# Batch 0's rows and spectra with the 32 slots innermost, batch 1's first stage moved behind the last stage of batch 0's transform, idle products on TensorE up to layer 1, and the last pieces of w2 decoded later

## The chip, the cores and the metric

The kernel runs on one core of one Trainium2 chip. The metric is the time of one execution on the device in microseconds (us); lower is better. Three runs of the kernel before took 1601.73, 1601.77 and 1603.76 us, so the median is 1601.77 us. The execution that the profiler recorded took 1600.86 us by the same clock.

The engines are called PE (TensorE, matrix products; its weight loads are PEld), DVE (VectorE), ACT (ScalarE), POOL (GpSimd) and SP (SyncE, which issues nearly all transfers). PSUM is the memory that PE writes and that ACT and DVE read; SBUF is the memory that all engines work from. A "unit-stride" walk reads neighbouring elements of a partition one after the other; a "strided" one jumps.

## The reference

Eight sequences of 3136 tokens with 256 features go through two parts, all in float32:

```
X  = rfft(x, axis=1)
Yr = Xr @ w_r - Xi @ w_i + b_r
Yi = Xr @ w_i + Xi @ w_r + b_i
Y  = soft_threshold(Yr, 0.01) + 1j * soft_threshold(Yi, 0.01)
y  = irfft(Y, n=3136)
u  = y + (y.T @ U @ V).T        # U: 3136 x 32, V: 32 x 3136
out = u + relu(u @ w_ch1) @ w_ch2   # 256 -> 1024 -> 256
```

U, V, w_ch1 and w_ch2 arrive as 64-bit floats and the kernel turns their words into float32 itself ("decoding").

## The kernel before, in words

**The stages.** The transform of 3136 = 49 x 64 points is done as small matrix products. For each batch, stage A is a product over 49 rows, stage B a product with twiddles (25 row pairs, called slots, which are handled two at a time), then the mix (the 256 x 256 products with w_r and w_i, bias and threshold), then C (the inverse of B) and D (the inverse of A, together with the product with U). The product with V and two layers follow: layer 1 (l1_chunks, seven products by a scheme that saves one of eight) and layer 2 (l2_chunks). Layer 1 and 2 run in 49 windows of 512 tokens, six per batch and one for what is left. While the windows of batch b run, the stages of batch b+1 are put between them. Most float32 products are done as three products of a high and a low part.

**Batch 0 is special.** It has no windows of an earlier batch to run beside. a_first (line 689) loads the rows of batch 0 in six pieces and does 16 products of 512 columns, each of which leaves 32 slots x 16 features in one PSUM bank. DVE turns each bank in blocks of 32 x 32 (STREAM_TRANSPOSE) into t0t (line 665), which is kept in SBUF. In t0t the feature index is innermost: one slot's 128 features are neighbours, so b_early and b_mm (lines 832, 843) load a slot as PE weights at unit stride, and the transposes write at a stride of 128 elements. C (c_unit, line 1002) writes its spectra back to t0t, features innermost, by a copy on ACT (line 1012). z_turn (line 1100) then turns t0t in 16 transposes of 512 elements into zz; it reads and writes at strides of 128 or 64 elements. D of batch 0 (d_unit, line 1122) loads 64 neighbouring features of zz as weights, 256 products, each in two passes on PE. Its 12 units (6 groups of rows times 2 halves of the features) write two PSUM banks each; ACT copies them to xq, DVE adds up the U part in pa.

**What is shared.** The tiles t0t and w1t (weights of layer 1) share one region of SBUF (tag "w1"), x3w, zz0 and w2t (weights of layer 2) another ("w2"). So w1t can be written only when z_turn has read t0t, and w2t only when D has read zz0.

**Other work at the start.** decode (line 1230) turns one piece of 512 words in about a dozen instructions on ACT, DVE and, for w2, POOL. decoding (line 1480) goes through V, U, the four pieces of w1, combine (line 1442, which makes the seven weight tiles of w1t) and the four pieces of w2; steps(n) takes n of its steps. make_ud (line 1375) makes the product of U with the inverse table: 128 small products and, on ACT, 24 small copies to du, which D reads. Stage A of batch 1 (a_mm, line 724; eight units in two halves of four) loads xt, does four tiled products per unit and writes the result to DRAM (gd), from where stage B of batch 1 loads it. a_half has its two halves recorded at 95 and 133 on the scale of line 1537.

**What sets the order.** Nothing runs in the order in which it is written. Each instruction is recorded with a cost (cost, line 195), dependencies and a place; order and forward (lines 263, 391) simulate the five engines, take at each moment the ready instruction with the earliest due time, and trace (line 529) emits each engine's queue in that order. Where forward expects a gap on PE ahead of the first product into a PSUM tile, it fills it with products of the identity with itself (line 540) into that tile; these are called idle products here, and they are planned only in the first 200 us. Line 545 makes each POOL tensor operation wait for the DVE operation on SBUF before it in the plan, since the two share ports.

**From D to layer 1.** p_spread and p_unit (lines 1190, 1198) reduce pa, turn it on PE and split it into pt. u_prep (line 1603) of window 0 then multiplies pt with V (psv), adds this to xq, forms differences in tt, and splits them into high parts on ACT (oah, obh, och, odh) and low parts on POOL (oal, obl, ocl, odl). Layer 1 starts on these.

Of the kernel before, what the change touches and what calls it, by code (L numbers as in the profile page):

```python
# [27 lines left out]
NI = 32  # L28
# [13 lines left out]
STEPS_W = 8  # L42
# [119 lines left out]
class _Op:  # L162
    __slots__ = "n eng name args kw out cost lag move port mode group lead fill start preds succs unit at".split()


class _Program:


    def __init__(self):
        self.ops = []  # L170
        self.group = None

# [22 lines left out]
    def cost(self, op, out, ins):  # L195
# [22 lines left out]
        elif op.eng == "act":  # L218
            op.cost = 0.062 + 0.000844 * n + (0.036 if sb else 0) + (0.098 if "bias" in op.kw else 0)
            op.lag = 0.2  # L220
# [42 lines left out]
    def order(self):  # L263
# [66 lines left out]
        for k, u in enumerate(units):  # L330
            u[0].fill = fill.get(k, 0)
            for op in u:
                op.start = starts[k] + op.at
# [57 lines left out]
    def forward(self, units, size, tags, gap, late):  # L391
# [52 lines left out]
        self.idle = []  # L444
        starts, fill = [0.0] * len(units), {}
        while done < len(units):
# [42 lines left out]
            if e == "pe":  # L489
# [4 lines left out]
                gap_, each = t - max(free[e], b.granted) - 0.2, 0.222  # L494
                if done_pe == 0:
# [3 lines left out]
                fill[k] = max(0, int(gap_ / each)) if b.first[0] is u and t < FILL else 0  # L499
# [29 lines left out]
    def trace(self, engines, junk, tc):  # L529
# [4 lines left out]
        for op in sorted(self.ops, key=lambda o: (o.start, o.n)):  # L534
            if op.fill:
                o = op.out.buf.get()
# [14 lines left out]
def fft_mix_moe_kernel(  # L551
# [28 lines left out]
    def psm(shape, name):  # L580

        turn_m[0] += 1
        k = turn_m[0] % 3
        return (ps_m if k < 2 else ps_o).tile(shape, F32, tag=("psm0", "psm1", "pso0")[k], name=name)

    def banks(turn, name):

        pools = ((ps_f, "psf"),) * 2
        if turn % 4 == 1:
            pools = (ps_m, "psm0"), (ps_m, "psm1")  # L590
        elif turn % 4 == 3:
            pools = (ps_o, "pso0"), (ps_o, "pso1")
# [65 lines left out]
    w1t = const.tile([128, 7, 2, 512], F32R, name="w1t", tag="w1")  # L658
# [6 lines left out]
    t0t = const.tile([128, 57 * 128], F32, name="t0t", tag="w1")  # L665
    t0 = [t0t[:, 3200 * h : 3200 * h + 4096].rearrange("p (k d) -> p k d", k=32) for h in range(2)]
# [22 lines left out]
    def a_first():  # L689
# [10 lines left out]
        for k, xt in enumerate(parts):  # L700
            ps = ps_f.tile([128, 512], F32, tag="psf", name=f"psa_0_{k}").rearrange("p (i d) -> p i d", i=NI)
            pe.matmul(ps, lhsT=fa0, rhs=xt, start=True, stop=True)
# [4 lines left out]
            dve.transpose(out=t0[h][:, :, d : d + 16].rearrange("p k d -> p d k"), in_=ps.rearrange("p i d -> p d i"))  # L707
# [16 lines left out]
    def a_mm(b, c, loads=()):  # L724
# [33 lines left out]
    def a_spread(b, lo, hi, behind=12):  # L758
        us = []
        for half in range(2):  # L760
# [31 lines left out]
    def load_fb(b, q):  # L792
# [5 lines left out]
        else:  # L798
            fbt = mp.tile([128, 2, 128], F32, tag="oc" + "hl"[q % 2], name=f"fb_{b}_{q}")
# [202 lines left out]
    def c_unit(b, q):  # L1002
# [97 lines left out]
    def z_turn(h, m):  # L1100
        if m == 0 and h == 0:
            t = const.tile([128, NI, 128], F32, name="zz0", tag="w2")
            zz.extend([t[:, :, 0:64], t[:, :, 64:128]])
        elif m == 0:
            zz.append(const.tile([128, NI, 64], F32, name="zz2", tag="wm"))
        elif m == 4 and h == 1:
            zz.append(qp.tile([128, NI, 64], F32, tag="xq", name="zz3", bufs=3))
# [14 lines left out]
    def d_unit(b, t, du, loads=(), hs=(0, 1)):  # L1122
# [75 lines left out]
    def p_unit(b):  # L1198
# [8 lines left out]
        pt = qp.tile([128, D], F32R, tag="pt", name=f"pt_{b}")  # L1207
# [22 lines left out]
    def decode(name, hi=None, lo=None, full=None):  # L1230
# [6 lines left out]
        q, lf, p2 = [  # L1237
            mp.tile([128, 512], U32, tag="sv", name="d%s_%s%d%d" % (tag, *name), bufs=4)[:pp, :n]
            for tag in "mlp"
        ]  # L1240
# [94 lines left out]
    def setup_w(wrs=wrs, wis=wis, wt=wt):  # L1335

        dve.scalar_tensor_tensor(
            out=wt, in0=wrs, scalar=-1.0, in1=wis, op0=ALU.mult, op1=ALU.subtract
        )
# [35 lines left out]
    def make_ud(t):  # L1375
        n0, n = UNITS_D[t]
        ps = psm([128, 512], f"psu_{t}")
        parts = [(64 * j + 32 * r, K1 * j + 25 * r, 25 - r) for j in range(2) for r in range(2)]
        for k in range(n):
            for p, c, m in parts:  # L1380
                pe.matmul(
# [7 lines left out]
                )  # L1389
        for p, _, m in parts:  # L1390
# [138 lines left out]
    for half in range(2):  # L1529
        loads = []  # L1530

        def load(c, half=half, loads=loads):
            loads += a_load(1, 4 * half + c)

        for c in range(4):
            on((92, 129)[half] + c / 10, load, c)
        on((95, 133)[half], lambda half=half, loads=loads: a_half(1, half, loads + [s_state["c"]]))
    on(99.5, wait_2)
    for n in range(16):
        on(100.5 + 2 * n, steps, 1)  # L1540

    def turn():
        steps(100)
# [59 lines left out]
    def u_prep(w):  # L1603
# [4 lines left out]
        lo_eng = pool  # L1608
# [4 lines left out]
        def pair(tag, src, n=2):  # L1613
# [3 lines left out]
                else mp.tile([128, HT], F32R, tag=f"oc{k}", name=f"{tag}{k}_{w}")  # L1617
# [27 lines left out]
        def s1():  # L1645
            sub(dve, tv[:, 0], b_[0][1], b_[0][0])
            sub(dve, tv[:, 1], b_[1][1], tv[:, 0])
            hl["a"] = pair("oa", tv)

        def s2():  # L1650
            hl["b"] = pair("ob", x[:, :, 0:8])
# [188 lines left out]
    for st in u0:  # L1840
        st()
    setup_w()
# [164 lines left out]
```

## Time and profile before

| | |
|---|---|
| median of three runs | 1601.77 us |
| the profiled execution, its time | 1600.86 us |
| its span, from the first to the last instruction | 1599.0 us |
| PE busy | 1573.2 us, 98% |
| DVE busy | 1278.7 us, 80% |
| ACT busy | 942.1 us, 59% |
| POOL busy | 441.2 us, 28% |
| share of PE in the chain that ended last | 87% |

The busy time of PE contains the idle products, so a busy PE is not always one at work. A row of the table by stretches gives the stretch, its length, busy time and number of instructions of each engine, the granted clock of TensorE as a share of 2.4 GHz (0.5 is 1.2 GHz), and what the transfer engines did. A float32 product that is not split runs as two passes, and each pass is one instruction in the trace.

### The profile page before, as it was taken

Reading aid. Unit: us, or ns where it says so; the run is one execution under the profiler, and the core shown is the slowest. Engines: PE = TensorE matmul, PEld = TensorE weight load, DVE = VectorE, ACT = ScalarE, POOL = GpSimd, SP = SyncE. Lnnn points to the kernel's source line nnn. Section 1 sums busy time; section 2 is a strip of 40 time slices with the busy share of each in tenths; the row PEclk is TensorE's granted clock in tenths of the full one; section 3 lists DMA queues with packets and bytes.
Section 4 is the critical chain, followed back from the end, with each engine's and each line's share of the span. In section 5 each row is a group of like instructions: output and inputs, shape, how many; then the busy total and the mean of one; then the engine's idle time right before and its main releaser. Section 6 shows DMA issues by size and latency. Waiting matters only on the chain.

```text
span 1599.0 us, 37615 instructions
## 1 busy us (share of the span) xinstructions
PE 1573.2 (98%) x14586; PEld 1415.6 (89%) x14586; DVE 1278.7 (80%) x2486; ACT 942.1 (59%) x1998; POOL 441.2 (28%) x417
## 2 busy tenths in 40 slices
PE   8989999999999999999999999999999999999998
PEld 6957899899889889899888988999978999999997
DVE  7878898679977788678986889768986789866775
ACT  3856666566655666556655666556665566554553
POOL 1305343133312333223331333223321233312221
PEclk9979999999999999999999999999999999999999
DMA  9655254617674454715574365523656134520332
GB/s 227 199 146 152 72 180 133 153 55 180 172 194 116 126 149 113 176 30 143 155 206 125 98 178 146 131 81 96 163 152 193 29 95 120 125 67 14 82 61 39
DMA packets 220501, 202.73 MB, mean 127 GB/s; under 512 B 127590, under 2 KB 192408, under 8 KB 220244
## 3 DMA queue, kind: packets, MB, share of 16 engines
q1 hardware_dynamic: 217686, 199.47, 46.6%
q8 instruction: 115, 1.88, 0.5%
q10 hardware_dynamic: 2638, 0.86, 0.3%
q14 instruction: 62, 0.51, 0.1%
HBM read 123.69 MB, written 78.60 MB: 127 GB/s over the span
## 4 chain that ended last, share of the span: by engine, by line
PE 87%; DVE 7%; issue 2%; ACT 1%; DMA 1%; POOL 0%; SPq 0%; DVEq 0%; ACTq 0%; POOLq 0%
PE pso L542 30%; PE psy L542 18%; PE psx L542 8%; PE psq L542 6%; PE psb L542 5%; PE psd L542 5%; PE psa L542 4%; PE psz L542 4%; PE psc L542 3%; PE pst L542 3%; DVE ys L542 1%; PE psv L542 1%; DVE zz L542 1%; DVE tb L542 1%; DVE rl L542 1%
## 5 line engine op out<-in xcount | busy, mean ns | idle before, releaser
L542 PE MATMUL pso<-rh,w2t 128*128 128x512 f32 x1568 | 405.4, 381 | 0.0
L542 PEld LDWEIGHTS pso<-rh,w2t 128*128 128x128 f32 x1568 | 274.4, 190 | 26.5
L542 PE MATMUL pso<-rl,w2t 128*128 128x512 f32 x784 | 233.3, 379 | 0.0
L542 POOL TENSOR_TENSOR yl<-ys,yh 128x512 fp32r<-128x512 f32 (+1 forms) x94 | 121.4, 1292 | 223.8 <-ACT yh L542 88.1
L542 ACT ACTIVATE rh<-s 128x512 fp32r<-128x512 f32 x196 | 122.3, 629 | 78.7 <-DVE s L542 74.5
L542 PEld LDWEIGHTS pso<-rl,w2t 128*128 128x128 f32 x784 | 148.2, 189 | 21.0
L542 DVE SCALAR_TENSOR_TENSOR rl<-s,rh 128x512 fp32r<-128x512 f32 x196 | 149.7, 767 | 18.4 <-ACT rh L542 16.2
L542 DVE SCALAR_TENSOR_TENSOR ys<-tb,rl 64x256 f32<-64x256 f32 x350 | 151.9, 434 | 14.7 <-ACT rl L542 9.4
L542 POOL TENSOR_TENSOR tl<-ts,th 128x256 fp32r<-128x256 f32 x88 | 65.7, 746 | 313.5 <-DVE ys L542 116.2
L542 PE MATMUL psq<-wmt,xsh 128*128 128x256 f32 (+1 forms) x704 | 123.3, 276 | 0.0
L542 PE MATMUL psy<-odh,w1t 128*128 128x256 f32 x784 | 123.2, 280 | 0.0
L542 PEld LDWEIGHTS psy<-odh,w1t 128*128 128x128 f32 x784 | 109.9, 191 | 11.1 <-DVE rl L542 1.6
L542 PEld LDWEIGHTS psq<-wmt,xsh 128*128 128x128 f32 (+1 forms) x704 | 109.4, 191 | 2.5 <-ACT xt L542 0.8
L542 POOL TENSOR_TENSOR obl<-xq,obh 128x512 fp32r<-128x512 f32 x48 | 61.5, 1281 | 173.1 <-DVE tt L542 56.9
L542 POOL TENSOR_TENSOR odl<-tt,odh 128x512 fp32r<-128x512 f32 x49 | 63.7, 1300 | 128.0 <-ACT odh L542 92.0
L542 DVE TENSOR_TENSOR s<-psz,s 128x512 f32<-128x512 f32 x98 | 67.0, 684 | 39.9 <-PE psz L542 22.7
L542 ACT ACTIVATE rh<-v 128x512 fp32r<-128x512 f32 x98 | 61.8, 631 | 61.8 <-DVE v L542 59.7
L542 PE MATMUL psq<-wmt,xsl 128*128 128x256 f32 (+1 forms) x352 | 96.8, 275 | 0.0
L542 DVE TENSOR_TENSOR v<-v,psy 128x512 f32<-128x512 f32 x98 | 66.7, 681 | 35.8 <-PE psy L542 17.1
L542 ACT ACTIVATE xq<-psd 128x294 f32<-128x294 f32 (+1 forms) x192 | 69.5, 440 | 42.2 <-PE psd L542 40.3
L542 PE MATMUL psb<-fb,t 128*128 128x128 f32 (+1 forms) x700 | 93.1, 276 | 0.1
L542 ACT ACTIVATE s<-psx 128x512 f32<-128x512 f32 x98 | 58.5, 597 | 56.5 <-PE psx L542 55.1
(218 smaller groups left out, 3954.7 us busy)
## 6 DMA issues: line engine op xcount, KB each, us to landing
gd<-xt SPq DMA_DIRECT2D x112, 224.0 KB
zt<-zd SPq DMA_DIRECT2D x112, 224.0 KB
out_dram<-os SPq DMA_DIRECT2D x190, 128.0 KB
xt<-in_x_dram SPq DMA_DIRECT2D x96, 224.0 KB
t<-gd SPq DMA_DIRECT2D x84, 256.0 KB
zd<-zs SPq DMA_DIRECT2D x84, 256.0 KB
fb<-in_fb_dram SPq DMA_DIRECT2D x96, 128.0 KB
vw<-vd SPq DMA_DIRECT2D x44, 256.0 KB
```

The lines of the kernel that those rows point to most:

```text
L542: made = call(*[real(a) for a in op.args], **{k: real(a) for k, a in op.kw.items()})
```

## The change

- t0t becomes two halves of 128 features x 32 slots with the slots innermost; zz gets the same order. A's products read their rows with a rearranged view (`p i d -> p d i`), so that the PSUM bank is already in the order of the transposes. B's and D's weight loads and C's copy now walk at a stride of 32 elements.
- Stage A of batch 1: the first half is recorded behind D (129 to 133), its copies all on ACT; the second half goes to the windows of batch 0 (a_spread, loads from step 0, products from step 6.5).
- Two idlers (one product each of the identity) mark a stretch, from the last C product to the first windows' preparation. In it forward fills every gap on PE with idle products into a tile of its own. make_ud for t above 0 waits for the first idler.
- steps: 5 instead of 8 at place 91, 6 at place 128 instead of 16 from 100.5 on; the rest comes after u_prep of window 0 and waits for its fourth step. setup_w waits for the third C product.
- For window 0 alone the low parts oal and obl are made on DVE. pt and oc move into the region of w1, tables of batch 0 from "oc" to "zs". Costs in the planner change.

```diff
-            slow = op.name == "transpose" and not sb
-            op.cost = 0.07 + (0.00053 if op.name == "tensor_scalar" else 0.00158 if slow else 0.00104) * n
+            op.cost = 0.07 + (0.00053 if op.name == "tensor_scalar" else 0.00104) * n
...
+                if idling:
+                    gap_ = t - free[e] - 0.2
+                if u in self.idlers:
+                    idling = not idling
...
-                fill[k] = max(0, int(gap_ / each)) if b.first[0] is u and t < FILL else 0
+                fill[k] = max(0, int(gap_ / each)) if (b.first[0] is u or idling) and t < FILL else 0
...
-    t0t = const.tile([128, 57 * 128], F32, name="t0t", tag="w1")
-    t0 = [t0t[:, 3200 * h : 3200 * h + 4096].rearrange("p (k d) -> p k d", k=32) for h in range(2)]
+    t0t = const.tile([128, 2, 128, 32], F32, name="t0t", tag="w1")
+    t0 = [t0t[:, h] for h in range(2)]
...
-            ps = ps_f.tile([128, 512], F32, tag="psf", name=f"psa_0_{k}").rearrange("p (i d) -> p i d", i=NI)
-            pe.matmul(ps, lhsT=fa0, rhs=xt, start=True, stop=True)
+            ps = ps_f.tile([128, 512], F32, tag="psf", name=f"psa_0_{k}").rearrange("p (d i) -> p d i", i=NI)
+            pe.matmul(ps, lhsT=fa0, rhs=xt.rearrange("p i d -> p d i"), start=True, stop=True)
...
-            dve.transpose(out=t0[h][:, :, d : d + 16].rearrange("p k d -> p d k"), in_=ps.rearrange("p i d -> p d i"))
+            dve.transpose(out=t0[h][:, d : d + 16], in_=ps)
...
-            if j:
+            if j and (b, c // 4) != (1, 0):
...
-            ts = [[t0[h][:, slot(k0 + k)] for h in range(2)] for k in range(n)]
+            ts = [[t0[h][:, :, slot(k0 + k)] for h in range(2)] for k in range(n)]
...
-            zv = t0t[:, 0:6400].rearrange("p (t k n) -> p k t n", t=2, k=25)[:, slot(k0) : slot(k0) + n]
+            zv = t0t.rearrange("p t n k -> p k t n")[:, slot(k0) : slot(k0) + n]
...
         dve.transpose(
-            out=zz[2 * h + e][:, :, d : d + 16].rearrange("p i d -> p d i"),
-            in_=t0[h][:, :, 16 * m : 16 * m + 16].rearrange("p k d -> p d k"),
+            out=zz[2 * h + e][:, d : d + 16], in_=t0[h][:, 16 * m : 16 * m + 16]
         )
...
-                return zz[2 * h + e][p, i]
+                return zz[2 * h + e][p, :, i]
...
+                if t > 0:
+                    mm.preds[prog.idlers[0].n] = prog.idlers[0]
...
-        on((95, 133)[half], lambda half=half, loads=loads: a_half(1, half, loads + [s_state["c"]]))
+    on(133, lambda: a_half(1, 0, loads))
     on(99.5, wait_2)
-    for n in range(16):
-        on(100.5 + 2 * n, steps, 1)
+    for n in range(6):
+        on(128 + n / 10, steps, 1)
+    idle = ps_o.tile([128, 128], F32, tag="pso0", name="idle")
+    def idler():
+        prog.idlers.append(pe.matmul(idle, lhsT=ident, rhs=ident, start=True, stop=True))
+        e = s_state.pop("c")
+        prog.idlers[-1].preds[e.n] = e
+    on(98, idler)
...
-            hl["a"] = pair("oa", tv)
+            hl["a"] = pair("oa", tv, 2, pool if w else dve)
...
+    first = s_state["c"]
+    idler()
+    n = len(prog.ops)
+    steps(100)
+    for op in prog.ops[n:]:
+        if op.eng in ("act", "dve"):
+            op.preds[first.n] = first
...
+                if b == 0:
+                    side += a_spread(1, -5, 5, 6.5, (1,))
```

## Rows read from the trace of the kernel before

**Rows 1.** The page of the profile: the span, and the granted clock of TensorE in 40 equal slices of it.

```profile
span 1599.0 us, 37615 instructions
...
PEclk9979999999999999999999999999999999999999
```

**Rows 2.** Busy time by stretches: start and end, length, then PE, PEld, DVE, ACT and POOL busy us (instructions), granted clock, share of the transfer engines, GB/s.

```profile
9.40:25.10 15.70, 15.55 (x42) 7.18 (x42) 14.38 (x16) 2.70 (x7) 3.20 (x3) 1.00 0.99 206
...
31.40:82.80 51.40, 51.40 (x421) 50.21 (x421) 43.60 (x71) 41.64 (x80) 14.90 (x11) 0.98 0.74 210
82.80:91.30 8.50, 5.21 (x238) 3.72 (x241) 5.10 (x8) 6.99 (x18) 1.69 (x2) 0.99 0.34 87
91.30:104.90 13.60, 12.92 (x82) 6.26 (x82) 11.97 (x13) 6.52 (x18) 0.00 (x0) 0.51 0.44 119
104.90:122.60 17.70, 14.26 (x519) 12.93 (x518) 14.24 (x32) 9.61 (x27) 2.62 (x3) 0.81 0.62 175
122.60:141.80 19.20, 18.27 (x139) 13.72 (x139) 17.77 (x35) 12.44 (x26) 9.44 (x8) 1.00 0.48 141
141.80:150.00 8.20, 7.00 (x51) 5.87 (x50) 4.98 (x9) 4.04 (x10) 8.11 (x7) 1.00 0.53 159
...
200.00:1500.00 1300.00, 1297.96 (x12103) 1177.79 (x12102) 1049.11 (x2101) 777.11 (x1658) 365.83 (x338) 1.00 0.47 127
...
91.30:141.80 50.50, 45.45 (x739) 32.90 (x739) 43.98 (x79) 28.57 (x69) 12.05 (x10) 0.80 0.52 147
```

**Rows 3.** The timeline of stage A of batch 0: start, length from the first to the last of the group, engine, instruction, count.

```profile
9.42 14.37 PE L542 MATMUL psa<-xx,fa 98*128 98x512 f32 x32 [1.57 <-DMA xx<-in_x_dram]
...
10.58 14.49 DVE L542 STREAM_TRANSPOSE t0t<-psa 128x512 f32<-128x512 f32 x16 [10.58 <-PE psa L542]
```

**Rows 4.** The three kinds of DVE transposes of 128 x 512, by their tiles: shortest, median and longest in ns, first and last start.

```profile
L542 DVE STREAM_TRANSPOSE t0t<-psa x16: 1001/1024/1054, 10.6 to 24.0; 128x512 f32<-128x512 f32 x16
L542 DVE STREAM_TRANSPOSE zz<-t0t x16: 1145/1193/1246, 92.9 to 112.8; 128x512 f32<-128x512 f32 x16
...
L542 DVE STREAM_TRANSPOSE os<-xq x96: 660/700/712, 181.2 to 1592.8; 128x512 f32<-128x512 f32 x96
```

**Rows 5.** ACT copies of 512 elements, by their tiles (columns as in rows 4): one that reads SBUF at a stride of 32 elements, one that reads it at unit stride, and C's copy from PSUM to t0t.

```profile
L542 ACT ACTIVATE vh<-v x2: 1132/1136/1141, 53.1 to 54.1; 96x512 fp32r<-96x512 f32 x2
...
L542 ACT ACTIVATE rh<-v x98: 612/631/657, 149.5 to 1580.8; 128x512 fp32r<-128x512 f32 x98
...
L542 ACT ACTIVATE t0t<-psc x13: 375/597/635, 40.4 to 92.3; 128x512 f32<-128x512 f32 x12, 128x256 f32<-128x256 f32 x1
```

**Rows 6.** The chain of work that ended last: start, length, engine, tile, count. Layer 2's products of 512 columns, whose moving operand alternates between two halves of a tile, and stage B's products of 128 columns with 128 x 128 weights.

```profile
149.19 0.89 PE psb L542 x8
...
153.91 1.30 PE pso L542 x6
```

**Rows 7.** The timeline of ACT around the last spectra of batch 0 (columns as in rows 3).

```profile
85.71 2.05 ACT L542 ACTIVATE du<-psu 25x192 f32<-25x192 f32 x6
...
92.30 0.60 ACT L542 ACTIVATE t0t<-psc 128x512 f32<-128x512 f32 x1
```

**Rows 8.** From the spectra to the end of D: DVE's and PE's timeline, the copies to du by their tile, and the products of D by stretch for batch 1 (columns as in rows 2, of these instructions alone, without POOL).

```profile
92.93 5.51 DVE L542 STREAM_TRANSPOSE zz<-t0t 128x512 f32<-128x512 f32 x5 [3.79 <-ACT t0t L542]
...
100.95 4.06 PE L540 MATMUL psd<-ident 128*128 128x128 f32 x18
104.94 3.05 PE L542 MATMUL psd<-du,zz 56*64 56x81 f32 x156
...
L542 ACT ACTIVATE du<-psu x24: 251/324/329, 85.7 to 96.6; 25x192 f32<-25x192 f32 x8, 24x192 f32<-24x192 f32 x8, 25x128 f32<-25x128 f32 x4, 24x128 f32<-24x128 f32 x4
...
293.00:323.50 30.50, 11.44 (x512) 9.95 (x512) 5.29 (x22) 8.54 (x24) 1.00 0.52 136
```

**Rows 9.** The timelines of DVE, ACT, PE and POOL from the end of D to the first products of layer 1.

```profile
124.33 0.43 DVE L542 TENSOR_TENSOR pr<-pa 128x256 f32<-128x256 f32 x1
...
128.00 0.43 DVE L542 TENSOR_TENSOR pt<-psp,pt 64x256 fp32r<-64x256 f32 x1
...
131.10 1.27 DVE L542 TENSOR_TENSOR xq<-xq,psv 128x512 f32<-128x512 f32 x2
...
134.32 0.63 ACT L542 ACTIVATE oah<-tt 128x512 fp32r<-128x512 f32 x1 [0.97 <-DVE tt L542]
...
131.42 8.87 PE L540 MATMUL psr<-ident 128*128 128x128 f32 x78
...
142.85 0.49 PE L542 MATMUL psx<-oal,w1t 128*128 128x256 f32 x2 [0.39 <-POOL oal L542]
...
140.29 1.28 POOL L542 TENSOR_TENSOR wmt<-wis,wmt 128x512 fp32r<-128x512 f32 x1 [6.75 <-DVE vr L542]
141.53 1.27 POOL L542 TENSOR_TENSOR oal<-tt,oah 128x512 fp32r<-128x512 f32 x1
```

**Rows 10.** Stretches again, for some instructions alone (PE, PEld, DVE and ACT as far as they have any, then the clock): one half of stage A of a later batch, stage B of batch 1, the decoding tile dm (DVE, ACT, POOL), and all engines in the first part of window 0.

```profile
184.00:189.00 5.00, 3.89 (x32) 1.18 (x32) 2.44 (x4) 2.20 (x4) 1.00 0.82 217
...
141.80:150.00 8.20, 2.03 (x16) 1.94 (x16) 0.61 (x3) 0.99 (x4) 1.00 0.53 159
...
122.60:141.80 19.20, 6.12 (x10) 2.09 (x3) 2.50 (x2) 1.00 0.48 141
...
150.00:166.00 16.00, 16.00 (x120) 15.21 (x120) 14.25 (x29) 9.36 (x21) 5.89 (x7) 1.00 0.45 126
```

More of the change, by code (lines that the diff above doesn't have):

```diff
@@ L37 @@
 NF = 8
-STEPS_W = 8
+STEPS_W = 5
 START = 22
@@ L162 @@
 class _Op:
-    __slots__ = "n eng name args kw out cost lag move port mode group lead fill start preds succs unit at".split()
+    __slots__ = "n eng name args kw out cost lag move port mode group lead fill start preds succs unit at wide".split()
 class _Program:
@@ L171, in __init__ @@
         self.group = None
+        self.idlers = []
     def engine(self, eng):
@@ L219, in cost @@
             op.cost = 0.062 + 0.000844 * n + (0.036 if sb else 0) + (0.098 if "bias" in op.kw else 0)
+            if ins and ins[0].dtype == U32 or out.shape[0] < 32:
+                op.cost += 0.13
             op.lag = 0.2
@@ L223, in cost @@
             op.port = sb and op.name != "transpose"
-            slow = op.name == "transpose" and not sb
-            op.cost = 0.07 + (0.00053 if op.name == "tensor_scalar" else 0.00158 if slow else 0.00104) * n
+            op.cost = 0.07 + (0.00053 if op.name == "tensor_scalar" else 0.00104) * n
+            if out.shape[0] == 64:
+                op.cost += 0.1
+            elif n < 128 and any(v.buf is out.buf for v in ins):
+                op.cost += 0.18
+            elif op.name == "tensor_scalar":
+                op.cost += 0.1
             op.lag = 0.185
@@ L331, in order @@
             u[0].fill = fill.get(k, 0)
+            u[0].wide = k in self.wide
             for op in u:
@@ L444, in forward @@
         self.idle = []
+        idling, wide = False, {}
+        self.wide = wide
         starts, fill = [0.0] * len(units), {}
@@ L498, in forward @@
                 done_pe += 1
-                fill[k] = max(0, int(gap_ / each)) if b.first[0] is u and t < FILL else 0
+                fill[k] = max(0, int(gap_ / each)) if (b.first[0] is u or idling) and t < FILL else 0
+                wide.pop(k, None)
+                if idling and fill[k]:
+                    wide[k] = True
             free[e] = t + sum(op.cost for op in units[k])
@@ L535, in trace @@
             if op.fill:
-                o = op.out.buf.get()
+                o = (self.idlers[0].out.buf if op.wide else op.out.buf).get()
                 while len(o.shape) > 2:
@@ L756, in a_half, with a_spread @@
             a_mm(b, 4 * half + c, loads if c == 0 else ())
-    def a_spread(b, lo, hi, behind=12):
+    def a_spread(b, lo, hi, behind=12, halves=(0, 1)):
         us = []
-        for half in range(2):
+        for half in halves:
             at = lo + (hi - lo) * half / 2
@@ L1235, in decode @@
         hw, lw = w[:, :, 1], w[:, :, 0]
[L1237 to L1240, printed above, removed]
+        if name[0] == 2 and name[1] % 2:
+            if "late" not in words:
+                words["late"] = mp.tile([128, 2, 512], U32, tag="rl", name="dp_2", bufs=3)
+            ml = mp.tile([128, 2, 512], U32, tag="rl", name="dm_%s%d%d" % name, bufs=3)
+            q, lf = ml[:, 0], ml[:, 1]
+            p2 = words["late"][:, name[1] // 2]
+        else:
+            q, lf, p2 = [
+                mp.tile([128, 512], U32, tag="sv", name="d%s_%s%d%d" % (tag, *name), bufs=4)[:pp, :n]
+                for tag in "mlp"
+            ]
         m = q
@@ L1335, in setup_w @@
     def setup_w(wrs=wrs, wis=wis, wt=wt):
+        e = s_state["c2"]
         dve.scalar_tensor_tensor(
             out=wt, in0=wrs, scalar=-1.0, in1=wis, op0=ALU.mult, op1=ALU.subtract
-        )
+        ).preds[e.n] = e
         sub(dve, wis, wis, wrs)
@@ L1380, in make_ud @@
             for p, c, m in parts:
-                pe.matmul(
+                mm = pe.matmul(
                     ps[p : p + m, R * k : R * k + R],
@@ L1528, in fft_mix_moe_kernel, with load @@
     on(91, steps, STEPS_W)
[L1529 to L1536, printed above, removed]
-        on((95, 133)[half], lambda half=half, loads=loads: a_half(1, half, loads + [s_state["c"]]))
-    on(99.5, wait_2)
-    for n in range(16):
-        on(100.5 + 2 * n, steps, 1)
+    loads = []
+    def load(c):
+        loads.extend(a_load(1, c))
+    for c in range(4):
+        on(129 + c / 10, load, c)
+    on(133, lambda: a_half(1, 0, loads))
+    on(99.5, wait_2)
+    for n in range(6):
[6 more added lines that the diff above has]
+    on(98, idler)
     def turn():
-        steps(100)
         p_spread(0)
@@ L1839, in fft_mix_moe_kernel @@
     u0 = u_prep(0)
-    for st in u0:
+    for k, st in enumerate(u0):
         st()
+        if k == 3:
+            s_state["c"] = prog.ops[-1]
+    first = s_state["c"]
[5 more added lines that the diff above has]
+            op.preds[first.n] = first
     setup_w()
```

34 lines of the change are left out of this document (17 added, 17 removed).

## The prediction, made before the changed kernel ran

> **What bounds the kernel now.** I looked at the granted clock over the span first, then at stretches, then at single instructions. The clock is full everywhere but at the start [rows 1], and from 200 to 1500 us PE is busy for 1297.96 of 1300 us [rows 2]: there is nothing to gain there, and whatever PE gets on top costs its full length. The first 150 us are another matter. Between 31.4 and 82.8 PE is busy without a break (stages B, mix and C). From 82.8 to 141.8 it isn't: the granted clock is 0.51 from 91.3 to 104.9 (the lower level, 1.2 GHz) and 0.81 in the next stretch, and much of the busy time is idle products: 78 of them, 8.87 us, in one go [rows 9]. The busiest engine there is DVE, with 43.98 of 50.5 us against 28.57 of ACT [rows 2]. So this stretch is set by DVE and by chains from engine to engine. The change works almost only there.
>
> **The sum, stage by stage.** All against the profiled execution: 1600.86 us, of which the span is 1599.0.
>
> *Stage A.* 32 passes take 14.37 us, 0.449 each, so 0.898 per bank; the 16 transposes take 14.49, 0.906 each, and the last ends at 25.07, 1.28 after PE's last product [rows 3]. They read PSUM and write SBUF at a stride and last 1.024 us; the transposes of the output, at unit stride in blocks of 32, last 0.700 [rows 4]. With these DVE no longer limits; PE does, at the same pace. The end comes 0.3 us sooner from the last transpose, and perhaps 0.4 from the pace: -0.7. The products now read their rows at a stride, of which no row shows the price. It lies between nothing (layer 2's moving operand jumps between two halves at every element, and 512 columns take 1.30/6 = 0.217 us [rows 6]) and what ACT pays for a read at a stride, 1.136 against 0.631, a factor of 1.8 [rows 5]: 0 to +11.5. I take 0, as the nearer row is one of PE.
>
> *B, mix, C.* 50 products with t0t as weights (25 slots, two halves), so 100 passes, now load them at a stride. Their pace is 0.89/8 = 0.111 [rows 6]; with the factor 1.8 as upper end +8.9, lower end 0, taken 0 for the same reason. C's 13 copies now write at a stride: from 0.597 up to 1.0 (the transposes that wrote at a stride [rows 4]), 5 us of ACT at most, in a stretch where ACT is busy 41.64 of 51.4 us [rows 2]; PE hides it, and if not it costs up to 3. Taken 0. At the end of C, ACT makes copies to du (2.05 us for six) while the last spectra wait [rows 7]; 20 of the 24 now come behind C's last product. This brings the last spectrum forward: -2.5 (0 to -4).
>
> *From the last spectrum to D.* Now 12.0 us: from 92.93 eight transposes at 1.193 and three copies of batch 1's stage A on DVE lie ahead of the first product of D at 104.94 [rows 4, 8]. Afterwards it is eight transposes at 0.70, 5.6 us, beside 20 copies to du at 0.32, 6.5 us [rows 8], which D now waits for as well, and an ACT copy and hand-overs of about one: 7.5. So -4.5. If the transposes stayed as slow, -1.5; with no wait for du, -6.
>
> *D.* 17.7 us today, at a clock of 0.81 with DVE still turning the second half. The same 512 passes take 11.44 us of PE in batch 1 at the full clock [rows 8]; idle products are to hold that clock. ACT's 24 copies (8.54) and DVE's adds (5.29) with eight transposes (5.6) fit beside it. I take 12.2, so -5.5 (0 to -7). D's weights are loaded at a stride too: 0 to +9 by the factor above (0.8 x 11.44), taken 0.
>
> *D to layer 1.* 122.6 to 142.85 today, 20.2 us. DVE finishes w1 and w2, then POOL makes wmt, having waited 6.75 us for one DVE instruction (vr), and only then oal at 141.53 [rows 9]. The chain itself is pa, pr 0.43, psp, two steps to pt (0.43 each), psv, xq 1.27, tt, oah 0.63, oal: 6 us of durations and ten hand-overs of some 0.2, about 8. oal and obl go from POOL (1.27) to DVE (some 0.7), and the later decoding is held behind them. But DVE and ACT set a floor. DVE: 43.98, less 7.9 for the 16 transposes, less 5.5 for the eight copies that go to ACT or into the windows, less 4.3 (seven decoding instructions of 0.61 [rows 10]), plus 1.4: 27.7. ACT: 28.57, plus 3.5 of copies to du, less 2.9 of decoding: 29. Both now have to fit between the last spectrum (89.7 after the gains so far) and layer 1, so 31 to 32 us at the best packing, and layer 1's first full product at 121: 11.5 us for this part, so -8.7 (-3 to -12).
>
> Together: -0.7 - 2.5 - 4.5 - 5.5 - 8.7 = -21.9 at layer 1.
>
> *Given back.* Four units of stage A of batch 1 leave a stretch in which PE had time for one in which it has none: 3.89 us of PE [rows 10]. Stage B of batch 1 can't start before this half is in DRAM and read again; its 16 passes between 141.8 and 150, 2.03 us today in gaps of layer 1 [rows 10], are done later at full price: +1.8. The first window starts with nothing beside it, and DVE, busy 14.25 of 16 us in it today [rows 10], gets the 4.3 of decoding and two splits more: +3 (0 to 6). Moved past SP: four units' loads and eight stores to DRAM, which now stand among those of window 0; PE's next work doesn't wait for them before stage B. Together +8.7 (4 to 12).
>
> The wait of setup_w for C and that of make_ud for the first idler are behind work that ends earlier anyway; behind the waiting make_ud on PE are only idle products and D, counted above. Behind the held decoding stand window 0's relu instructions only by due time, not by position. Idle products that are planned too long would hold PE at most one of 0.23 us per gap (8.87/39).
>
> Sum: -21.9 + 8.7 = -13.2. Profiled time 1600.86 - 13.2 = 1587.7; the median of the runs lies 0.9 above the profiled time, so 1588.6.
>
> **A rule that speaks against it.** The trace shows that ACT needs 1.8 times as long for a read at a stride of 32 elements [rows 5]; no row shows PE so. The Trainium skill's page "SBUF — State Buffer", section "Door 1: The DMA port swizzle", says that SBUF is served in lines of 16 bytes and that each access to a new line costs extra, without excepting an engine. ACT's rows agree with it; the alternating operand of layer 2 [rows 6] does not show such a cost on PE. If it held for PE, the first rival below would come true.
>
> **Rivals.**
> 1. *TensorE pays for the stride.* For: ACT's rows 5, and that the old zz transposes, strided on both sides, need 1.193 against 0.700 [rows 4]. Against: rows 6. All three places are on the path: A +11.5, B +8.9, D +6 (the middle of 0 to 9, as four tiles share the loads) = +26.4. With -13.2 this gives +13.2: 1615. It turns slower from about half of that, a factor of 1.4. Chance 0.11.
> 2. *ACT and DVE take the stretch back.* Each has 28 to 29 us of work where I allow 31 to 32; a due time set wrongly puts decoding, wmt or the low parts ahead of the chain, as POOL's 6.75 us show [rows 9]. Layer 1 then comes at 126 to 130 and the first window gives back 10: -1 to -7, in the middle 1597.5. Chance 0.19, a third of it within 0.2% of before.
> 3. *The transposes don't get faster* (bound by their block order, not by the stride): -7.9 is lost from the 16 of zz, of which about five on the path: 1594. Against: the 96 of the output. Chance 0.08.
> 4. *Little is given back*: window 0 hides the decoding, and stage A of batch 1 falls in gaps of layer 1's start. Given back 3 instead of 8.7, and D nearer to its lower end: -20, 1582. Chance 0.12.
>
> **The numbers.** My forecast, 1588.6 with 1583 to 1594 as its own range, has 0.50. 0.2% of the time is 3.2 us, about what a measurement of this kernel can tell from no change. Faster by more: 0.50 + 0.08 + 0.12 + two thirds of rival 2 (0.13) = 0.83; the same 0.06; slower 0.11. The range from 1579 to 1600 takes in the forecast, rival 3, most of rivals 2 and 4, and leaves out rival 1.
>
> **What would show it.** Transposes t0t and zz near 0.70 us; products of stage A still at 0.449 a pass and stage B's at 0.111; first product of D some 13 us earlier and D in 12 us; granted clock 1.0 from 91 us to layer 1; layer 1's first products with oal near 121; a half of psa (32 passes, 3.9 us) in window 0; the tail from 200 us as before, only earlier. Wrong would be: a pass of stage A at 0.8 us, C's copies at 1.0 with PE waiting for them, or layer 1 later than 130.

## The result and the profile after

The changed kernel takes 1614.46 us (median of four runs, 1613.26 to 1616.28) against 1601.99 of the kernel before (four runs). The ratio is 1.0076, with an interval of 1.0059 to 1.0094: it is slower by 12.5 us, where 13.2 us of gain were forecast. The profiled execution is at 1616.28, its span 1614.5.

I split both spans at the same points: the start of ACT's copy of the last spectrum, D's first product, D's last product, and layer 1's first product on the low and high parts (its first with `oah` or `obh`). The changes add up to +15.5, the difference of the two spans.

| stretch, us | before | after | change | forecast |
|---|---|---|---|---|
| start to the last spectrum's copy | 92.30 | 110.77 | +18.5 | -3.2 |
| from there to D's first product | 12.64 | 8.00 | -4.6 | -4.5 |
| D, first to last product | 17.61 | 20.07 | +2.5 | -5.5 |
| D's end to layer 1's first product | 19.22 | 12.05 | -7.2 | -8.7 |
| layer 1's first product to the end | 1457.2 | 1463.6 | +6.4 | +8.7 |

Two of the five lines are far off, and both are stretches in which TensorE reads what now lies at a stride. These are the busy times by stretches of the changed kernel, with the columns of [rows 2]; the last three stretches are from the last spectrum's copy to D, D, and from D to layer 1.

```profile
9.40:25.10 15.70, 15.65 (x19) 4.24 (x20) 5.74 (x8) 3.84 (x11) 3.24 (x3) 0.89 0.97 219
25.10:31.40 6.30, 6.30 (x9) 1.56 (x8) 2.87 (x4) 0.06 (x1) 0.00 (x0) 1.00 0.00 0
31.40:82.80 51.40, 50.61 (x295) 44.52 (x294) 34.62 (x63) 32.65 (x65) 9.45 (x7) 0.93 0.54 150
...
200.00:1500.00 1300.00, 1296.79 (x12101) 1176.88 (x12094) 1051.20 (x2101) 773.13 (x1657) 369.01 (x338) 1.00 0.47 127
110.80:118.80 8.00, 6.27 (x234) 5.02 (x233) 6.91 (x12) 6.62 (x20) 0.00 (x0) 0.93 0.58 164
118.80:138.90 20.10, 20.10 (x536) 19.41 (x536) 12.19 (x34) 13.50 (x34) 4.03 (x3) 0.93 0.24 64
138.90:150.90 12.00, 11.81 (x87) 7.55 (x87) 7.90 (x19) 9.32 (x20) 5.63 (x5) 1.00 0.51 156
```

In the first stretch PE is as busy as before, 15.65 against 15.55 us, but with 19 instructions in place of 42. In 31.4 to 82.8 (stage A now reaches to 37.2) it is 295 in place of 421, and DVE and ACT each have 9 us less to do there: for the most part they wait for PE, which holds the chain of work up to 72.85 us. The granted clock, 0.89 in the first stretch, is not the cause: from 25.1 to 31.4 us it is 1.00, and the passes of stage A start 0.86 us apart there, as in the first. In D, PE is busy from end to end and its loader nearly so. Busy share alone would not have told this; the count beside it does. From 200 to 1500 us little has changed.

The instructions by their tiles say which ones became longer (shortest, median, longest in ns, first and last start):

```profile
L560 PEld LDWEIGHTS psb<-fb,t0t x100: 288/313/313, 37.1 to 92.9; 128*128 128x128 f32 x96, 64*128 64x128 f32 x4
...
L560 DVE STREAM_TRANSPOSE t0t<-psa x16: 716/717/718, 11.5 to 37.3; 128x512 f32<-128x512 f32 x16
L560 DVE STREAM_TRANSPOSE zz<-t0t x16: 667/668/711, 111.9 to 123.9; 128x512 f32<-128x512 f32 x16
L560 ACT ACTIVATE t0t<-psc x13: 608/1092/1130, 53.9 to 110.8; 128x512 f32<-128x512 f32 x12, 128x256 f32<-128x256 f32 x1
...
L560 PE MATMUL psa<-xx,fa x32: 1035/1037/1105, 9.5 to 36.2; 98*128 98x512 f32 x32
...
L560 PEld LDWEIGHTS psd<-du,zz x512: 185/222/237, 118.8 to 138.5; 56*64 56x64 f32 x171
```

The transposes are at 0.717 and 0.668 us, as forecast (1.024 and 1.193 before, [rows 4]). C's copy is at 1.092 against 0.597 [rows 5]. A pass of stage A lasts 1.037 us but the next one starts before it ends, so its price is read from the pace instead. That stands in the chain of the work that ended last (start, length, what, count):

```profile
9.45 27.76 PE psa L560 x32
...
64.20 5.18 PE psb L560 x24
...
110.77 1.09 ACT t0t L560
...
118.84 4.34 PE psd L560 x120
123.18 1.76 PE idle L558 x14
124.94 4.18 PE psd L560 x113
129.12 0.64 PE idle L558 x4
129.76 5.70 PE psd L560 x165
```

Stage A takes 27.76/32 = 0.867 us a pass, against 0.449 [rows 3]: +13.4 us in all. Stage B takes 5.18/24 = 0.216 a pass, against 0.111 [rows 6]: 100 passes are +10.5 us. The chain goes through D as products and idle products without a gap, so there PE sets the time; 3.0 us of it are idle products, which the plan put where it expected gaps.

### The profile page after: what moved, and what is told of

It reads as the page before. It is cut to its first block, busy times and chain, and to the rows that moved or that the text cites. A ratio compares the mean times of both kernels' runs of the same rounds, so it can differ in the third digit from the quotient of the medians.

```text
span 1614.5 us, 37566 instructions
## 1 busy us (share of the span) xinstructions
PE 1593.8 (99%) x14568; PEld 1430.1 (89%) x14568; DVE 1268.2 (79%) x2484; ACT 948.1 (59%) x2002; POOL 445.1 (28%) x415
## 4 chain that ended last, share of the span: by engine, by line
PE 90%; DVE 4%; ACT 2%; DMA 1%; issue 1%; POOL 1%; SPq 0%; DVEq 0%; POOLq 0%; ACTq 0%
PE pso L560 30%; PE psy L560 17%; PE psx L560 8%; PE psq L560 7%; PE psd L560 6%; PE psb L560 6%; PE psa L560 5%; PE psz L560 4%; PE psc L560 3%; PE pst L560 3%; PE psv L560 1%; DVE ys L560 1%; DVE rl L560 1%; DMA xx<-in_x_dram 1%; DVE tb L560 0%
## 5 line engine op out<-in xcount | busy, mean ns | idle before, releaser
L560 DVE SCALAR_TENSOR_TENSOR ys<-tb,rl 64x256 f32<-64x256 f32 x350 | 157.9, 451 | 13.8 <-ACT rl L560 8.3
L560 DVE SCALAR_TENSOR_TENSOR rl<-s,rh 128x512 fp32r<-128x512 f32 x196 | 151.7, 777 | 18.6 <-ACT rh L560 16.6
L560 PE MATMUL psy<-odh,w1x 128*128 128x256 f32 x784 | 122.4, 279 | 0.8 <-issue 0.8
L560 PEld LDWEIGHTS psy<-odh,w1x 128*128 128x128 f32 x784 | 110.3, 191 | 12.1 <-issue 5.0
```

What stands on the lines that cost most here:

```text
L560: made = call(*[real(a) for a in op.args], **{k: real(a) for k, a in op.kw.items()})
```

## The experiments

### The layout without the rest, and the rest without the layout

The first kernel is the change with the old order of t0t and zz (features innermost, strided transposes); the second is the kernel before with nothing but the new order and the places in SBUF that go with it.

```diff
e1_rest_old_layout, on the changed kernel
-    t0t = const.tile([128, 2, 128, 32], F32, name="t0t", tag="w1")
+    t0t = const.tile([128, 57 * 128], F32, name="t0t", tag="w1")
...
-            pe.matmul(ps, lhsT=fa0, rhs=xt.rearrange("p i d -> p d i"), start=True, stop=True)
+            pe.matmul(ps, lhsT=fa0, rhs=xt, start=True, stop=True)
...
-                return zz[2 * h + e][p, :, i]
+                return zz[2 * h + e][p, i]
e2_layout_only, on the kernel before
-                return zz[2 * h + e][p, i]
+                return zz[2 * h + e][p, :, i]
...
```

> The changed kernel with the old order of t0t and zz (features innermost, stage A's products at unit stride, transposes at a stride); everything else of the change stays. Theory S (TensorE pays for every load and operand that it reads at a stride, and this alone made the change slower): stage A's passes back at 0.449 us instead of 0.867 (-13.4 us), stage B's 100 passes at 0.111, C's copies at 0.6; zz transposes back at 1.19 (+8 us, some five on the path). Layer 1 some 14 to 20 us earlier than in the changed kernel, time 1592 to 1600. Rival O (the new order of the work - the idle products, stage A of batch 1 behind D, decoding held back - costs by itself, because the planner's costs no longer fit): 1605 or more, slower than before.

> The kernel before with only the slots-innermost order of t0t and zz (and the places of pt, oc and four tables that it needs to fit); idle products, stage A of batch 1, decoding and planner as before. Theory S: stage A +13.4 us, stage B about +11, D some +3 to +5, against -8 to -10 from the zz transposes: 1612 to 1622, slower than the changed kernel or like it. Rival O: the order alone is about neutral, 1595 to 1606.

The rest alone took 1594.88 us, 0.9961 of before (0.9947 to 0.9976): about 6 us faster. The layout alone took 1623.9, 1.0143 (1.0128 to 1.0158): 23 us slower, a little over the expected 1612 to 1622, with layer 1 at 164.58 in place of 141.77. In its trace the two kinds of TensorE reads are where they are in the changed kernel:

```profile
L542 PE MATMUL psa<-xx,fa x32: 1035/1037/1107, 9.9 to 36.6; 98*128 98x512 f32 x32
...
L542 PEld LDWEIGHTS psb<-fb,t0t x100: 288/313/315, 37.6 to 90.8; 128*128 128x128 f32 x96, 64*128 64x128 f32 x4
```

So the whole loss, and more, is the layout's; the other parts of the change help.

### Stage A's operand at unit stride

```diff
e3_a_unit, on the changed kernel
-            ps = ps_f.tile([128, 512], F32, tag="psf", name=f"psa_0_{k}").rearrange("p (d i) -> p d i", i=NI)
-            pe.matmul(ps, lhsT=fa0, rhs=xt.rearrange("p i d -> p d i"), start=True, stop=True)
+            ps = ps_f.tile([128, 512], F32, tag="psf", name=f"psa_0_{k}").rearrange("p (i d) -> p i d", i=NI)
+            pe.matmul(ps, lhsT=fa0, rhs=xt, start=True, stop=True)
...
-            dve.transpose(out=t0[h][:, d : d + 16], in_=ps)
+            dve.transpose(out=t0[h][:, d : d + 16], in_=ps.rearrange("p i d -> p d i"))
```

> The changed kernel with one thing undone: stage A's products read their rows at unit stride again (PSUM slots outermost), and the transposes read PSUM at a stride of 16 elements and write SBUF at unit stride. Theory S: a pass at 0.449 us, the last transpose of stage A near 25 us instead of 38, time 1600 to 1603, that is -12 to -14 against the changed kernel; the transposes 0.7 to 0.9. If the slow passes came from something else (late rows, PSUM banks held by the transposes), they stay at 0.87 and the time at 1614.

1601.64 us, 1.0005 of before (0.9996 to 1.0015): 12.8 us less than the changed kernel, for the 13.4 that stage A was worth. The products of A start from 9.1 to 22.5 us, and the transposes still take 0.717: they now read PSUM at a stride and write SBUF at unit stride. B, C and D are as in the changed kernel (313, 1100 and 220 ns).

### Two slots innermost: eight bytes a step

If the price belongs to the jump and not to the order, a layout in which two slots lie side by side could keep the fast transposes and give TensorE a step of 8 bytes.

```diff
e4_pairs_innermost, on the changed kernel (and stage A as in e3_a_unit)
-    t0t = const.tile([128, 2, 128, 32], F32, name="t0t", tag="w1")
+    t0t = const.tile([128, 2, 16, 128, 2], F32, name="t0t", tag="w1")
...
-            ts = [[t0[h][:, :, slot(k0 + k)] for h in range(2)] for k in range(n)]
+            ts = [[t0[h][:, slot(k0 + k) // 2, :, slot(k0 + k) % 2] for h in range(2)] for k in range(n)]
...
-                return zz[2 * h + e][p, :, i]
+                return zz[2 * h + e][p, i // 2, :, i % 2]
...
```

> The changed kernel with two slots innermost instead of 32 (t0t and zz as 16 slot pairs x features x 2), stage A's products at unit stride. Weights for B and D are loaded at a stride of 2 elements, the transposes walk pairs of neighbours, C's copy writes pairs. Theory L (what costs is a step to another line of SBUF with every element; two hits in each 16 bytes are enough): transposes 0.70 us, stage B's passes 0.111, D's loads 0.133, C's copies 0.6; time 1583 to 1592, faster than both kernels. Rival N (any step that is not one slows TensorE): B's passes and D's loads stay near 0.2 us, time 1600 to 1605. Rival D (the transposes need 32 neighbours): they stay near 1.0 us, time 1592 to 1600.

1587.16 us (1581.33 to 1589.85), 0.9909 of before (0.9884 to 0.9933): nearly the time that was forecast for the change itself. Its instructions by tile, beside those of the changed kernel above:

```profile
L560 PEld LDWEIGHTS psb<-fb,t0t x100: 190/196/198, 23.5 to 71.5; 128*128 128x128 f32 x96, 64*128 64x128 f32 x4
...
L560 DVE STREAM_TRANSPOSE t0t<-psa x16: 669/717/719, 10.5 to 24.4; 128x512 f32<-128x512 f32 x16
L560 DVE STREAM_TRANSPOSE zz<-t0t x16: 669/670/712, 87.9 to 96.9; 128x512 f32<-128x512 f32 x16
L560 ACT ACTIVATE t0t<-psc x13: 397/597/608, 39.6 to 87.2; 128x512 f32<-128x512 f32 x12, 128x256 f32<-128x256 f32 x1
...
L560 PEld LDWEIGHTS psd<-du,zz x512: 132/135/228, 92.9 to 109.7; 56*64 56x64 f32 x171
```

Loads of B at 196 ns in place of 313, of D at 135 in place of 222, C's copies at 597 in place of 1092, and the transposes as fast. Against the changed kernel, layer 1's first product comes 27.7 us earlier (123.17 against 150.89) and the median is 27.3 lower. The terms of PE measured above, 13.4 for A, 10.5 for B and 5.3 for D (its 512 passes are 17.25 us of PE against 11.94), are 29.2. That the two lie so near is partly chance: D is only 2.8 us shorter (17.3 against 20.1), as waits take up part of what its passes save, while the way from the last spectrum to D, 2.3 us shorter, is not among the terms.

### The same layout in the kernel before

```diff
e5_before_pairs, on the kernel before
-    t0t = const.tile([128, 57 * 128], F32, name="t0t", tag="w1")
+    t0t = const.tile([128, 2, 16, 128, 2], F32, name="t0t", tag="w1")
...
```

> The kernel before with the pair order of t0t and zz alone (two slots innermost, and the places it needs); idle products, stage A of batch 1, decoding and planner as before. Theory L plus a DVE-bound start: the transposes fall to 0.7 us, stage B and D keep their pace, so DVE gets some 8 us back between 91 and 142 us and layer 1 starts 3 to 7 us earlier: 1594 to 1598. Rival (layer 1 waits for POOL and the decoding, not for the transposes): 1599 to 1602, no gain without the rest of the change.

With the pairs alone the kernel before takes 1596.54 us, 0.9969 (0.9956 to 0.9982). Its profiled execution has layer 1 at 134.57, 7.2 us earlier, and 1457.2 us from there to the end, as before: nothing is given back. The transposes are thus worth about 4 us by the medians and the rest of the change 6, and together they give some 14. That they help each other beyond their sum is not shown: in the profiled executions layer 1 comes 7.2 us earlier by the transposes alone, 12.1 by the rest alone and 18.6 by both, and the intervals allow a plain sum too. Where the slow transposes cost their time when the rest is there can be read in D of the first experiment. The columns are start, length, engine, instruction, count, and the idle time ahead of it:

```profile
93.34 0.35 PE L560 MATMUL psd<-du,zz 56*64 56x81 f32 x2
96.79 3.56 PE L560 MATMUL psd<-du,zz 56*64 56x81 f32 x126 [3.10 <-DVE zz L560]
104.48 0.36 PE L560 MATMUL psd<-du,zz 56*64 56x81 f32 x4 [1.86 <-DVE pa L560]
105.69 4.58 PE L560 MATMUL psd<-du,zz 56*64 56x81 f32 x124 [0.85 <-DVE pa L560]
```

There D comes early and finds DVE still at the transposes: 3.10 us of waiting for zz and 2.71 for the adds behind them. It lasts from 93.34 to 117.45, 24.1 us.

### Four slots innermost, and stage A in pairs of features

Two more kernels ask where the price begins. The first puts four slots side by side, so that a step is 16 bytes; the second takes the changed kernel and lets A's operand read two neighbouring features before each jump.

```diff
e8_four_innermost, on e4_pairs_innermost
-    t0t = const.tile([128, 2, 16, 128, 2], F32, name="t0t", tag="w1")
+    t0t = const.tile([128, 2, 8, 128, 4], F32, name="t0t", tag="w1")
...
e9_a_pairs_of_features, on the changed kernel
-            pe.matmul(ps, lhsT=fa0, rhs=xt.rearrange("p i d -> p d i"), start=True, stop=True)
+            pe.matmul(ps, lhsT=fa0, rhs=xt.rearrange("p i (a q) -> p a i q", q=2), start=True, stop=True)
...
```

> The version with pairs innermost, with four slots innermost instead of two: weights for B and D at a stride of 4 elements, that is 16 bytes, so each element lies in another line of 16 bytes; the transposes walk runs of four. Theory L (lines of 16 bytes, two hits needed): stage B's passes at 0.2 us and D's loads at 0.22 as with a stride of 128 bytes, transposes 0.7, C's copies 0.6 or up to 1.1; time 1594 to 1602. Rival (only long jumps cost, 64 bytes and more): passes at 0.111, time like the version with pairs.

> The changed kernel (32 slots innermost), but stage A's moving operand takes two neighbouring features at a time before it jumps to the next row (p i (a q) -> p a i q with q = 2), and the transposes read PSUM at a stride of 2 elements. Stage B and D as in the changed kernel. Theory L for the moving operand (two hits in each 16 bytes are enough): passes of stage A at 0.43 to 0.45 us instead of 0.867, time 1600 to 1604 as with the unit-stride operand. Rival N (each jump costs, so half the jumps cost half): passes near 0.65 us, time 1606 to 1609.

With four slots innermost:

```profile
L560 PEld LDWEIGHTS psb<-fb,t0t x100: 305/329/332, 23.2 to 80.6; 128*128 128x128 f32 x96, 64*128 64x128 f32 x4
...
L560 DVE STREAM_TRANSPOSE zz<-t0t x16: 668/669/711, 97.6 to 107.4; 128x512 f32<-128x512 f32 x16
L560 ACT ACTIVATE t0t<-psc x13: 607/757/816, 40.7 to 96.9; 128x512 f32<-128x512 f32 x12, 128x256 f32<-128x256 f32 x1
```

A step of 16 bytes costs the weight loads as much as one of 128 (329 against 313 ns), while the transposes don't care. C's copy, which here writes two of every four neighbours, takes 757 ns. The kernel took 1598.70 us in its one run. With A in pairs of features:

```profile
L560 PE MATMUL psa<-xx,fa x32: 590/590/697, 9.4 to 22.9; 98*128 98x512 f32 x32
```

The 32 passes take 14.05 us again, the full pace, and the kernel 1601.57 in its one run, as e3_a_unit. So two elements in 16 bytes are enough for the full pace, as neighbours in the moving operand and as every second one in a weight load. One alone takes 0.867/0.449 = 1.93 times as long as a moving operand (from one start to the next 0.860 against 0.430 us, twice). Where only the weights are read so, as in stage B, a pass takes 0.216/0.111 = 1.95 times as long; the load's own duration grows from 192 to 313 ns.

The Trainium skill's page "SBUF — State Buffer", section "Door 1: The DMA port swizzle", says that SBUF is served in lines of 16 bytes, that each access to a new line costs extra, and that a pattern should use each line at least twice. The pairs and the fours agree with it, on TensorE's operands too (weight loads of 196 and 329 ns). Layer 2's operand [rows 6], which changes line with every element, shows no such cost, so the elements of a line need not be read one right after the other there.

### The other parts, one at a time, on the pair layout

```diff
e6_pairs_no_idle
-                if u in self.idlers:
-                    idling = not idling
e7_pairs_half_in_setup: both halves of batch 1's stage A at the start
-    on(133, lambda: a_half(1, 0, loads))
+        on((95, 133)[half], lambda half=half, loads=loads: a_half(1, half, loads + ([] if half else [s_state["c"]])))
...
-                if b == 0:
-                    side += a_spread(1, -5, 5, 6.5, (1,))
e10_pairs_decode_before: all of w2 decoded ahead of window 0
-    for n in range(6):
-        on(128 + n / 10, steps, 1)
+    for n in range(12):
+        on(128 + n / 20, steps, 1)
```

> The version with pairs innermost, but the planner doesn't fill gaps between the last C product and window 0 with idle products (those ahead of the first product into a tile stay). Theory (the clock matters): the granted clock falls to 0.5 to 0.8 between 88 and 123 us, D's 512 products take 14 us instead of 12, layer 1 starts 2 to 5 us later: 1589 to 1592. Rival (D waits for ACT and DVE anyway): the same time within 1.5 us although the clock falls.

Without the idle products the time is 1590.67 us (ten runs, 1588.1 to 1598.63), 0.9948 (0.9934 to 0.9963); the interval lies just above that with them. The theory that they bring layer 1 forward falls: it comes at 119.20, 4 us earlier than with them, 2.6 of which are there already at the last spectrum's copy, ahead of nearly all of them. Their effect on the clock is there. Stretches of this kernel, from the last spectra to D, D, and from D to layer 1 (columns as in [rows 2]), and one later:

```profile
84.70:91.30 6.60, 4.11 (x180) 3.32 (x168) 6.02 (x12) 6.16 (x21) 1.27 (x1) 0.77 0.64 179
91.30:107.40 16.10, 13.73 (x521) 12.59 (x520) 12.84 (x35) 12.26 (x34) 3.99 (x3) 0.88 0.37 100
107.40:119.20 11.80, 11.14 (x78) 6.87 (x79) 8.17 (x20) 9.26 (x21) 5.61 (x5) 1.00 0.53 160
...
1020.00:1040.00 20.00, 16.43 (x259) 14.37 (x259) 9.35 (x22) 7.87 (x18) 1.58 (x2) 0.83 0.61 166
```

and the same three of the kernel with idle products:

```profile
87.20:92.90 5.70, 5.17 (x199) 4.25 (x189) 5.10 (x10) 5.33 (x18) 1.27 (x1) 1.00 0.55 171
92.90:110.20 17.30, 14.81 (x537) 13.29 (x535) 13.93 (x37) 13.46 (x36) 3.97 (x3) 0.96 0.39 105
110.20:123.20 13.00, 12.81 (x88) 8.44 (x87) 7.91 (x19) 9.47 (x20) 5.64 (x5) 0.93 0.47 147
```

The clock is 1.00 and 0.96 with them, 0.77 and 0.88 without, yet D is not shorter with them (17.3 against 16.1 us). One reason stands in the chain of the work that ended last, in D of the kernel with them:

```profile
95.93 1.76 PE idle L558 x14
...
101.15 0.64 PE idle L558 x4
...
107.33 0.64 PE idle L558 x4
```

Idle products are 3.0 us of this chain, waits 2.5 and D's own products 11.7. What the kernel without them loses, it loses later: in its profiled execution, which is at the median, 1469.7 us pass from layer 1 to the end against 1463.5. All of that is lost at one place, D of a later batch:

```profile
1030.57 1.07 PE L558 MATMUL psd<-dt,zt 49*64 49x81 f32 x19 [2.68 <-issue]
```

With a wait of 0.90 some 8 us before it PE loses 3.6 us there, and the clock is 0.83 in those 20 us. Counted from layer 1's first product, the output transposes come up to 1.5 us earlier than with idle products ahead of this place, and 5.8 us later behind it. "Issue" names no releaser; loads of dt and zt are issued just ahead of it, so a late transfer is likely, but that is not shown, nor whether it is so in every execution. What the idle products are worth stays open: from the last spectrum to layer 1 the execution with them is 1.4 us longer, while the medians are 3.5 in their favour.

> The version with pairs innermost, but both halves of stage A of batch 1 stay in the start, at the places of the kernel before (ahead of D and behind it); none is left for window 0. Theory G (the half costs its full 3.9 us in the windows, but 4 to 6 us of PE, ACT and DVE in the start): within 2 us of the version with pairs, 1585 to 1590. Rival (the start has free PE time, so the move was a loss): 1582 to 1584.

1589.29 us, 0.9925 (0.9910 to 0.9940), no difference that the intervals would show. Layer 1 comes 3.5 us later (126.67), and the rest takes 3.1 less (1460.4). The half is 3.9 us of PE [rows 10] wherever it stands.

> The version with pairs innermost, with all of w2 decoded ahead of window 0 (12 steps at place 128 instead of 6). Theory H (the held-back decoding shortens the way to layer 1 and is paid in window 0, where DVE is busy): layer 1 starts 0 to 4 us later than at 123.2 us, the time from there to the end falls by as much from 1463.5 us: 1585 to 1590, no clear difference to the version with pairs. Rival (holding it back is a gain by itself): 1591 or more.

1584.86 us (1583.4 to 1585.22), 0.9901 (0.9884 to 0.9917), just under the expected 1585 to 1590. Layer 1 comes at 123.60, only 0.4 later (1.5 counted from the last spectrum), though six more steps of the decoding stand ahead of it, and the rest takes 4.2 us less in the profiled execution (1459.3). By the interval it equals e4_pairs_innermost; it has the lowest median of all, and both beat both kernels.

## Why the prediction was wrong

**The step that failed: strided reads of TensorE taken as 0.** The prediction had the terms and their upper ends: A 0 to +11.5, B 0 to +8.9, D 0 to +9. They measured +13.4, +10.5 and +5.3 us of PE, 29.2 in place of 0. It took 0 three times because "the nearer row is one of PE", layer 2's operand that alternates between two halves [rows 6]. That was the wrong row. Two streams that each advance by one element still use all the neighbours, if in turns; a walk at a stride of 32 (B and D), or of 96 and 64 (A, the width of its tiles), uses one element and leaves the rest. That this is the difference is a reading of the pairs and the fours; no run changes layer 2's operand. ACT's row was the nearer one though it is of another engine: its factor is 1.8 [rows 5], and A measured 1.93.

**The first rival came true.** "TensorE pays for the stride" had 1615, with A +11.5, B +8.9 and D +6 on top of the forecast; 1614.46 was measured. Its mechanism is what the runs show; that its sum is right to a microsecond is partly luck. A and B cost 3.5 us more than it had, the stride lengthens D by 2.8 us for its 6 (20.1 against 17.3 with pairs), and the 5.5 us that D was to gain are there in neither layout. Its chance, 0.11, hung on the wrong row, and the range left it out.

**C's copies taken as 0.** They went to 1.092, a little over the upper end of 1.0. Four of the thirteen stand in the chain of waits of the changed kernel (1.02, 0.96, 0.95 and 1.09 us), which is 1.6 us more than four at 0.597, within the 0 to 3 that the prediction allowed. No run has them slow alone; the pair layout has them at 0.597. Where B's loads are slow in both, the last spectrum's copy starts at 96.95 us with copies of 1.100 (e3_a_unit) and at 96.91 with 0.757 (e8_four_innermost), so no price of theirs is seen there, though two executions could hide a microsecond of it.

**The transposes were right, the way to D in its number.** 0.717 and 0.668 us against a forecast of 0.70, and -4.6 us from the last spectrum to D against -4.5. The second is partly luck: with the same plan this way takes 5.7 us with pairs and 8.3 in e9_a_pairs_of_features. And the prediction had only -1.5 there if the transposes stayed slow; with slow ones (e1_rest_old_layout) the way takes 6.0 us, -6.6, and their time comes back as waits inside D.

**D was mis-sized even without the stride.** The forecast was 12.2 us, -5.5. In the pair layout, where loads are at full pace, D takes 17.27, only 0.3 less than before. Its products are 11.7 us of the chain, near the 11.44 that the forecast went by; idle products add 3.0 and waits 2.5. The prediction had idle products that are planned too long at "at most one of 0.23 us per gap"; here 14 passes, 1.76 us, stand in one go. DVE is busy 13.93 and ACT 13.46 of 17.3 us: decoding and what else the planner put in stand beside the copies and adds. The idle products raise the clock, but D is 1.2 us shorter without them.

**D to layer 1** came to -7.2 in the changed kernel and -6.3 with pairs, for -8.7. What the start gained more before D makes up for a part: with pairs the last spectrum's copy starts 5.1 us earlier (forecast -3.2) and D follows 5.7 us after it. Layer 1 comes 18.6 us earlier in all, for a forecast of 21.9.

**Given back:** +6.4 (6.3 with pairs) for +8.7. The likely parts are the half of stage A, of which e7_pairs_half_in_setup returns 3.1 us (3.9 forecast), and the held-back decoding, of which e10_pairs_decode_before returns 4.2, each in one profiled execution. With pairs the two errors nearly cancel: -18.6 + 6.3 = -12.3 in the profiled executions and -13.7 by the medians (1587.16 against 1600.83), for a forecast of -13.2. The gain that was forecast is there with another layout, but not from where it was forecast: D gives next to nothing of it.

## What to carry to other kernels

When an operand of TensorE is laid out anew, price its read by how many of the elements in 16 bytes it uses, and take the nearest row by that pattern, not by the engine; alternating streams say nothing of a stride. A layout need not be the one that suits the transpose or the one that suits TensorE: two elements side by side suited both here. An unknown that enters three terms on the path is one bet and not three, and deserves the weight of their sum in the range.

## What the runs showed that I had not expected

- TensorE's operands slow down at once and not by degrees: weight loads of 128 columns at 192 ns with steps of 4 bytes, 196 at 8, 329 at 16 and 313 at 128. ACT's write of C has a step between: 597 ns for neighbours, 757 for two of every four, 1092 for single elements at 128 bytes.
- DVE's transposes don't need unit stride: 0.67 to 0.72 us with two, four or 32 slots side by side, 1.02 to 1.19 only with the features innermost.
- A PE that is starved by its operand looks busier, not idler: in D 20.10 of 20.10 us (24 of the 536 instructions there are idle products), and 1593.8 us over the span against 1573.2 before.
